# A 64-step recurrence on one core: from stationary weights to stationary tokens in four column tiles, with a new split between resident and streamed weights

## Chip, cores, metric

One core of one Trainium2 chip. The metric is the device time of one execution in microseconds, the median of four runs. The program uses one core, and all runs named here were in the undisturbed (fast) state.

## The reference

The output is `g * a + (1 - g) * b` for 2048 tokens of width 1024. `b` is a feed-forward network with gate, width 3584. `g` is a sigmoid per token. `a` is a recurrence: 64 segments of 32 tokens are taken in order, and each is joined with 8 memory tokens that the segment before it produced.

```python
for s in range(64):
    xs = x[:, s*32:(s+1)*32]
    h = concat([mem, xs])                      # 40 tokens x 1024
    q, k, v = h @ Wq, h @ Wk, h @ Wv           # 32 heads of 128 -> 4096 columns each
    scores = q k^T / sqrt(128), masked         # 40 x 40 per head
    o = softmax(scores) v
    o = o @ Wo                                 # 4096 -> 1024
    mem = o[:8];  outs.append(o[8:])
```

The four weight matrices hold 33.5 MB in bf16. Every segment needs all of them and neither kernel keeps all of them on chip, so every segment streams some of them again. Only the 8 memory tokens tie one segment to the next: queries, keys and values of the 32 input tokens could be computed earlier, and outputs of tokens that feed no memory could be computed later.

One warning about correctness: the recurrence is a tiny part of the output. With `Wo` set to zero, the reference changes by 5.6e-6 on average, where its mean magnitude is 3.8e-3. The comparison with the reference therefore cannot judge the recurrence. So no run here shows that the recurrence of the changed kernel is computed right.

## The kernel before

Weights are the stationary operand (loaded ahead of each matmul, 128x128 values), and the 40 tokens move through it. Wq, Wo and a part of Wk stay in SBUF, the on-chip memory. Wv and the rest of Wk are streamed each segment through a ring of three slabs of 1 MB (four heads, rows of 1 KB).

```python
def emit_slab(i):                              # SP queue, in order
    ...
    slot = i % RING                            # RING = 3
    waits = [(S_QKV_DONE, slab_free_target[i - RING])]
    E("sp", lambda e: e.dma_start(ring[:, slot, :, :], slab_src(kind, hq)), ...)

# Q, K, V: 96 blocks of 8 matmuls per segment, weights 128x128 stationary, 40 columns moving
for kc in range(KC):
    ins = e.matmul(PB[bank][:, bi*L:(bi+1)*L], lhsT=lhs_list[kc],
                   rhs=hT[:, cur, kc, :], start=(kc == 0), stop=(kc == KC - 1))
...
# output projection, 8 x 32 matmuls per segment
for kc in range(H):
    ins = e.matmul(dst_bank[:, fl*L:(fl+1)*L], lhsT=wo_sb[:, kc, f*128:(f+1)*128],
                   rhs=oT_sb[:, kc, :], start=(kc == 0), stop=(kc == H - 1))
```

After the recurrence, the feed-forward part works through 8 row groups of 256 tokens. It streams gate and up weights from SP's queue, and fetches each group's recurrence output with one DMA from POOL's queue:

```python
E("pool", lambda e: e.dma_start(a_sb[:, :, :],
    a_scr[r0:r0 + RG*128, :].rearrange("(t p) f -> p t f", p=128)), waits=aw, inc=(S2_ALD, 16))
```

Of the kernel before, what the change touches and what calls it, by code (L numbers as in the profile page):

```python
# [5 lines left out]
BF16 = mybir.dt.bfloat16  # L6
FP32 = mybir.dt.float32
# [4 lines left out]

class _Sem:

    def __init__(self, h):
        self.h = h
        self.n = 0


class _Gen:  # L20
# [3 lines left out]
    def __init__(self):  # L24
        self.prog = {e: [] for e in self.ENGS}

    def emit(self, eng, mk, waits=(), inc=None):
        waits = tuple((s.h, int(t)) for (s, t) in waits if t > 0)
        if inc is not None:
            s, k = inc  # L30
            s.n += k
            inc_h = (s.h, k)
        else:
            inc_h = None

        def run(e, mk=mk, waits=waits, inc_h=inc_h):
            for sh, t in waits:
                e.wait_ge(sh, t)
            ins = mk(e)
            if inc_h is not None:  # L40
                ins.then_inc(inc_h[0], inc_h[1])

        self.prog[eng].append(run)

    def wait_only(self, eng, sem, target):
        if target <= 0:
            return

        def run(e, sh=sem.h, t=int(target)):
            e.wait_ge(sh, t)  # L50

        self.prog[eng].append(run)

    def materialize(self, block):
        prog = self.prog

        if prog["sp"]:
            @block.sync
            def _(e):
                for f in prog["sp"]:  # L60
                    f(e)

        if prog["pool"]:
            @block.gpsimd
            def _(e):
                for f in prog["pool"]:
                    f(e)

        if prog["pe"]:
            @block.tensor  # L70
            def _(e):
                for f in prog["pe"]:
                    f(e)

        if prog["act"]:
            @block.scalar
            def _(e):
                for f in prog["act"]:
                    f(e)

        if prog["dve"]:
            @block.vector
            def _(e):
                for f in prog["dve"]:
                    f(e)


def bass_gated_mix__memory_aug_recurrent_mem_tr__geglu_ffn__prompt_kernel(
# [17 lines left out]
    Dw, H, Dh = A_Wq.shape  # L106
    assert Dw == D and Dh == 128
    M = A_mem0.shape[1]
    SEG = 32
    assert M == 8  # L110
    L = M + SEG
    NSEG = S // SEG
    KC = D // 128
    F = H * Dh
    FF = B_w_gate.shape[1]
    NJ = FF // 128
    assert FF % 128 == 0 and D % 128 == 0 and S % 128 == 0
    NF = D // 128
    scale = float(Dh) ** -0.5
    NEG = -30000.0  # L120

# [3 lines left out]
    HG = 8 if H % 8 == 0 else H  # L125
    NG_ATT = H // HG
    assert H % 4 == 0
    NQG = H // 4

    KRES_H = min(H, 12)  # L130
    KRES_H -= KRES_H % 4
    RING = 3

    gen_all_sems = []

    with ExitStack() as es_top:
        cnt = [0]

        def new_sem(name):
            cnt[0] += 1  # L140
            h = es_top.enter_context(nc.semaphore(f"{name}_{cnt[0]}"))
            return _Sem(h)

        a_scr = nc.dram_tensor("a_scr_rows", [S, D], BF16)

        with ExitStack() as es:
            tcnt = [0]

            def SB(shape, dt, name):
                tcnt[0] += 1  # L150
                return es.enter_context(nc.sbuf_tensor(f"{name}_{tcnt[0]}", list(shape), dt))

            def PS(shape, dt, name):
                tcnt[0] += 1
                return es.enter_context(nc.psum_tensor(f"{name}_{tcnt[0]}", list(shape), dt))

            assert HG == 8 and NG_ATT * 8 == H, "v2 chain assumes 8-head attention groups"
            RING = 3
            hT = SB([128, 2, KC, L], BF16, "hT")
            stage = SB([128, D], BF16, "stage")  # L160
            qkvT = SB([128, 2, 24, L], BF16, "qkvT")
            v_sb = SB([L, 2, HG, 128], BF16, "vsb")
            sm = SB([L, 2, HG, L], FP32, "sm")
            pn = SB([L, 2, HG, L], BF16, "pn")
            mx = SB([L, 2], FP32, "mx")
            nmx = SB([L, 2], FP32, "nmx")
            rsum = SB([L, 2, HG], FP32, "rsum")
            rrec = SB([L, 2, HG], FP32, "rrec")
            pT_sb = SB([L, 2, HG, L], BF16, "pT")
            oT_sb = SB([128, H, L], BF16, "oT")  # L170
            a_evac = SB([128, NF, SEG], BF16, "aev")
            ident = SB([128, 128], BF16, "ident")
            mask = SB([L, HG, L], BF16, "mask")
            wq_sb = SB([128, KC, F], BF16, "wq")
            wo_sb = SB([128, H, D], BF16, "wo")
            ring = SB([128, RING, KC, 512], BF16, "ring")
            avail = nc.sbuf_bytes_remaining - 2048
            KRES_H = min(H, 4 * (avail // (KC * 512 * 2)))
            KRES_H = max(0, KRES_H - KRES_H % 4)
            kres_sb = SB([128, KC, max(KRES_H, 4) * 128], BF16, "kres") if KRES_H > 0 else None  # L180

            PB = [PS([128, 512], FP32, f"pb{i}") for i in range(8)]
            PBV = [PB[i][:, :].bitcast(BF16) for i in range(8)]

            S_CONST = new_sem("const")
            S_XLOAD = new_sem("xload")
            S_WQ = [new_sem(f"wq{i}") for i in range(H // 4)]
            S_KRES = [new_sem(f"kr{i}") for i in range(max(1, KRES_H // 4))]
            S_WO = new_sem("wo")
            S_SLOT = [new_sem(f"slot{i}") for i in range(RING)]  # L190
            S_QKV_DONE = new_sem("qkvdone")
            S_QKV_EVAC = new_sem("qkvevac")
            S_PINIT = new_sem("pinit")
            S_XTR_DONE = new_sem("xtrdone")
            S_HT = new_sem("htready")
            S_VTR_DONE = new_sem("vtrdone")
            S_VTR_EVAC = new_sem("vtrevac")
            S_SC_DONE = new_sem("scdone")
            S_SMRD = new_sem("smrd")
            S_NMX = new_sem("nmx")  # L200
            S_EXP = new_sem("exp")
            S_PN = new_sem("pn")
            S_PT_DONE = new_sem("ptdone")
            S_PT_EVAC = new_sem("ptevac")
            S_O_DONE = new_sem("odone")
            S_O_EVAC = new_sem("oevac")
            S_WO_DONE = new_sem("wodone")
            S_WOEV = new_sem("woev")
            S_ATR_DONE = new_sem("atrdone")
            S_ASTG = new_sem("astg")  # L210
            S_ASTORE = new_sem("astore")
            S_DVE_L = new_sem("dvel")
            S_POOL_L = new_sem("pooll")

            g = _Gen()
            E = g.emit

            E("pool", lambda e: e.memset(ident[:], 0.0), inc=(S_POOL_L, 1))
            E("pool", lambda e: e.affine_select(out=ident[:], in_=ident[:], compare_op=ALU.not_equal,
                                                fill=1.0, base=0, pattern=[[-1, 128]], channel_multiplier=1),  # L220
              waits=[(S_POOL_L, S_POOL_L.n)], inc=(S_CONST, 1))
            E("pool", lambda e: e.memset(mask[:], 0.0), inc=(S_POOL_L, 1))
            E("pool", lambda e: e.affine_select(
                out=mask[:, :, 0:SEG], in_=mask[:, :, 0:SEG], compare_op=ALU.is_ge,
                fill=NEG, base=0, pattern=[[0, HG], [-1, SEG]], channel_multiplier=1),
              waits=[(S_POOL_L, S_POOL_L.n)], inc=(S_POOL_L, 1))
            E("pool", lambda e: e.memset(mask[SEG:L], 0.0), waits=[(S_POOL_L, S_POOL_L.n)], inc=(S_CONST, 1))
            CONST_ALL = S_CONST.n

            E("pool", lambda e: e.dma_start(stage[32:64, :], xf[0:SEG, :]), inc=(S_XLOAD, 16))  # L230
            E("pool", lambda e: e.dma_start(stage[64:64 + M, :], mem0[:, :]), inc=(S_XLOAD, 16))

            chunk_plan = []
            for gq in range(NG_ATT - 1):
                chunk_plan.append((list(range(8 * gq, 8 * gq + 4)), ("k", "q", "v")))
                chunk_plan.append((list(range(8 * gq + 4, 8 * gq + 8)), ("k", "q", "v")))
            gL = NG_ATT - 1
            chunk_plan.append((list(range(8 * gL, 8 * gL + 6)), ("k", "q")))
            chunk_plan.append((list(range(8 * gL + 6, 8 * gL + 8)), ("k", "q")))
            chunk_plan.append((list(range(8 * gL, 8 * gL + 8)), ("v",)))  # L240
            NCH = len(chunk_plan)

            def chunk_blocks(ci):
# [804 lines left out]
```

## Time and profile before

| | before |
|---|---|
| time, median (range) | 4275.2 us (4262.6 to 4291.5) |
| period of a segment (63 periods) | 55.1 us |
| of it: TensorE busy / waiting for the ring / "issue" | 40.6 / 8.6 / 3.5 us |
| granted TensorE clock in the recurrence | 0.73 |
| streamed per segment | 12 slabs, 12.6 MB |
| a feed-forward row group | 75.7 us |

The page of the profiled run, with the engines' busy time and the span in 40 slices (digits are tenths):

```profile
PE 3214.3 (75%) x79512; PEld 2888.8 (68%) x79512; DVE 1113.6 (26%) x2577; ACT 933.5 (22%) x3010; POOL 82.0 (2%) x165
...
PE   3777777777777777677777777777777775899998
...
PEclk7777777767777777776776777777777776899999
DMA  9777777777777777677777777777777776666665
GB/s 326 223 224 238 224 238 231 235 232 234 234 238 241 241 232 233 217 237 225 240 233 230 231 228 233 231 241 241 241 241 225 237 235 205 204 212 207 207 207 167
```

No engine and no queue is full: TensorE is busy for about 0.7 of the recurrence, its granted clock is 0.73 of full on average, and the DMA queue moves about 233 GB/s at 0.74 of its time. (In the clock records the value is 1.0 or 0.5, nothing between; a mean of 0.73 says that TensorE ran at half clock for about 54% of the time.) When something is serial, one has to look inside a segment. The timeline of the kernel before (start, duration, engine, line, operation, count, and in brackets the idle time before and what ended it):

```profile
2003.90 0.36 PE L615 MATMUL pb_21<-hT,wq 128*128 128x40 bf16 x8
2004.10 0.36 PE L615 MATMUL pb_21<-hT,ring 128*128 128x40 bf16 x8
...
2008.82 0.23 PE L615 MATMUL pb_21<-hT,wq 128*128 128x40 bf16 x3
2011.98 0.33 PE L615 MATMUL pb_21<-hT,wq 128*128 128x40 bf16 x5 [2.93 <-issue]
...
2026.47 0.71 PE L615 MATMUL pb_20<-hT,ring 128*128 128x40 bf16 x16 [2.36 <-DMA ring<-in_A_Wv_dram]
```

Eight pairs of weight load and matmul start every 0.206 us at full clock, 25.7 ns each. At 2008.8 TensorE stops for 2.9 us with no wait that the profile shows ("issue"). Late instructions are the likely cause, though not proved: the packed trace has a 16 KB transfer on an instruction queue from 2009.4 to 2010.5. In 58 of the 71 such gaps of over 1 us between 200 and 2600 us a transfer of this kind ends inside the gap, mostly 1.3 to 1.5 us before TensorE goes on (a stretch of that length holds such an end by chance about half the time). At 2026 it has waited 2.4 us for a slab.

Two feed-forward row groups, in the chain that ended last, restricted to a window around them (start, duration, what):

```profile
4113.22 1.23 DVE dsb L992
...
4188.96 1.23 DVE dsb L992
```

The first subtraction of each row group comes 75.74 us after that of the last one.

### The profile page before, as it was taken

The page shows a single profiled execution, that of the slowest core. Times are in us where ns is not written, and L with a number is a line of the kernel's source. Part 1 is how long each engine was busy: PE and PEld are TensorE (multiplying, and loading weights), DVE is VectorE, ACT ScalarE, POOL GpSimd, SP SyncE. Part 2 cuts the span into 40 slices and gives each one's busy share as a digit, 9 for nine tenths or more (in the row PEclk, how much of TensorE's full clock was granted, in tenths as well). Part 3 has the DMA queues.
Part 4 walks back from the last instruction along what each step waited for, and adds up shares of the span by engine and source line. Part 5 has one row for each costly group of instructions (what it writes and reads, how often), then busy time and mean ns, then how long its engine had stood idle before and what let it go on. Part 6 is the DMA issues. An engine that isn't in the chain of part 4 may idle for free. (4 is left out here: it accounts for less than half of the span.)

```text
span 4275.1 us, 169326 instructions
## 1 busy us (share of the span) xinstructions
PE 3214.3 (75%) x79512; PEld 2888.8 (68%) x79512; DVE 1113.6 (26%) x2577; ACT 933.5 (22%) x3010; POOL 82.0 (2%) x165
## 2 busy tenths in 40 slices
PE   3777777777777777677777777777777775899998
PEld 3666666667666666666666666666766765677776
DVE  1122222222222222122222222222222221455555
ACT  1122222222222222122222222222222221232222
POOL 0000000000000000000000000000000000000000
PEclk7777777767777777776776777777777776899999
DMA  9777777777777777677777777777777776666665
GB/s 326 223 224 238 224 238 231 235 232 234 234 238 241 241 232 233 217 237 225 240 233 230 231 228 233 231 241 241 241 241 225 237 235 205 204 212 207 207 207 167
DMA packets 945190, 982.94 MB, mean 230 GB/s; under 512 B 17256, under 2 KB 930664, under 8 KB 944496
## 3 DMA queue, kind: packets, MB, share of 16 engines
q1 hardware_dynamic: 937904, 955.31, 70.2%
q0 software_dynamic: 6592, 16.81, 1.2%
q8 instruction: 627, 10.27, 1.0%
q14 instruction: 67, 0.55, 0.0%
HBM read 963.66 MB, written 8.39 MB: 227 GB/s over the span
## 5 line engine op out<-in xcount | busy, mean ns | idle before, releaser
L615 PE MATMUL pb_21<-hT,ring 128*128 128x40 bf16 x12288 | 557.9, 192 | 331.7 <-DMA ring<-in_A_Wv_dram 197.2
L615 PE MATMUL pb_20<-hT,ring 128*128 128x40 bf16 x12288 | 555.7, 192 | 315.6 <-DMA ring<-in_A_Wv_dram 173.6
L615 PEld LDWEIGHTS pb_21<-hT,ring 128*128 128x128 bf16 x12288 | 449.9, 105 | 359.4 <-DMA ring<-in_A_Wv_dram 207.1
L615 PEld LDWEIGHTS pb_20<-hT,ring 128*128 128x128 bf16 x12288 | 448.7, 104 | 349.6 <-DMA ring<-in_A_Wv_dram 183.9
L615 PE MATMUL pb_20<-hT,wq 128*128 128x40 bf16 x8192 | 402.5, 189 | 23.6 <-issue 23.3
L615 PE MATMUL pb_21<-hT,wq 128*128 128x40 bf16 x8192 | 401.4, 189 | 15.4 <-issue 15.1
L641 ACT ACTIVATE qkvT<-pb_21 128x160 bf16<-128x160 f32 (+3 forms) x736 | 179.4, 310 | 909.4 <-PE pb_21 L615 909.0
L641 ACT ACTIVATE qkvT<-pb_20 128x160 bf16<-128x160 f32 (+3 forms) x736 | 179.4, 310 | 890.6 <-PE pb_20 L615 890.2
L410 DVE SCALAR_TENSOR_TENSOR sm<-pb_25,mask 40x320 f32<-40x320 f32 x128 | 61.8, 483 | 1173.0 <-PE pb_25 L399 1173.0
L615 PEld LDWEIGHTS pb_20<-hT,wq 128*128 128x128 bf16 x8192 | 312.3, 102 | 24.8 <-issue 24.5
L615 PEld LDWEIGHTS pb_21<-hT,wq 128*128 128x128 bf16 x8192 | 311.9, 102 | 19.7 <-issue 19.4
L678 PE MATMUL pb_27<-oT,wo 128*128 128x40 bf16 x8192 | 277.3, 199 | 46.7 <-issue 33.0
L678 PE MATMUL pb_26<-oT,wo 128*128 128x40 bf16 x8192 | 256.3, 190 | 73.1 <-issue 73.1
L678 PEld LDWEIGHTS pb_27<-oT,wo 128*128 128x128 bf16 x8192 | 268.4, 109 | 55.1 <-issue 34.7
L678 PEld LDWEIGHTS pb_26<-oT,wo 128*128 128x128 bf16 x8192 | 246.5, 103 | 77.4 <-issue 77.2
L550 DVE COPY stage<-pb_22 32x1024 bf16<-32x1024 bf16 x64 | 43.5, 679 | 933.8 <-PE pb_22 L543 933.8
L969 PE MATMUL psB<-wd,GT 128*128 128x512 bf16 x896 | 228.7, 379 | 16.8 <-DVE GT L950 16.8
L451 PE MATMUL pb_23<-ident,qkvT 128*40 128x128 bf16 x2048 | 226.3, 278 | 15.0 <-issue 5.4
L907 PE MATMUL psh<-xTall,ringb 128*128 128x256 bf16 x1792 | 233.8, 274 | 0.6 <-DVE gall L870 0.6
L917 PE MATMUL psh<-xTall,ringb 128*128 128x256 bf16 x1792 | 233.2, 273 | 0.0
L907 PEld LDWEIGHTS psh<-xTall,ringb 128*128 128x128 bf16 x1792 | 176.0, 98 | 65.8 <-issue 0.6
L615 PE MATMUL pb_21<-hT,kres 128*128 128x40 bf16 x4096 | 192.0, 183 | 27.0 <-issue 17.7
(78 smaller groups left out, 3379.0 us busy)
## 6 DMA issues: line engine op xcount, KB each, us to landing
ring<-in_A_Wv_dram SPq DMA_DIRECT2D x512, 1024.0 KB, 6.1
ring<-in_A_Wk_dram SPq DMA_DIRECT2D x256, 1024.0 KB, 6.5
ringb<-in_B_w_gate_dram SPq DMA_DIRECT2D x56, 1024.0 KB, 5.2
ringb<-in_B_w_up_dram SPq DMA_DIRECT2D x56, 1024.0 KB, 7.8
wq<-in_A_Wq_dram SPq DMA_DIRECT2D x8, 1024.0 KB, 11.9
wo<-in_A_Wo_dram SPq DMA_DIRECT2D x8, 1024.0 KB, 13.9
wd<-in_B_w_down_dram SPq DMA_DIRECT2D x7, 1024.0 KB, 7.5
kres<-in_A_Wk_dram SPq DMA_DIRECT2D x4, 1024.0 KB, 11.6
```

The source lines that it names most:

```text
L410: E("dve", lambda e, b=b: e.scalar_tensor_tensor(out=sm[:, b, :, :], in0=PB[5 + b][0:L, 0:8 * L].rearrange("p (h k) -> p h k", h=8), scala ...
L451: ins = e.transpose(PBV[3][0:L, i * 128:(i + 1) * 128], qkvT[:, slot, 16 + i, :], ident[:, :])
L550: E("dve", lambda e: e.tensor_copy(stage[0:SEG, :], PBV[2][0:SEG, 0:D]), waits=dw, inc=(S_ASTG, 1))
L615: ins = e.matmul(PB[bank][:, bi * L:(bi + 1) * L], lhsT=lhs_list[kc], rhs=hT[:, cur, kc, :], start=(kc == 0), stop=(kc == KC - 1))
L641: E("act", lambda e, v3=v3, slot=slot, mi=mi, m=m, hh0=hh0, nh=nh: e.activation(qkvT[:, slot, midx[m] * 8 + hh0:midx[m] * 8 + hh0 + nh, :] ...
L678: ins = e.matmul(dst_bank[:, fl * L:(fl + 1) * L], lhsT=wo_sb[:, kc, f * 128:(f + 1) * 128], rhs=oT_sb[:, kc, :], start=(kc == 0), stop=(k ...
L907: ins = e.matmul(ps_h[:, hb, 0:RG * 128], lhsT=ringb[:, i_g % RINGB, kc, col:col + 128], rhs=xT_all[:, kc, rows], start=(kc == 0), stop=(k ...
L917: ins = e.matmul(ps_h[:, hb, RG * 128:2 * RG * 128], lhsT=ringb[:, i_u % RINGB, kc, col:col + 128], rhs=xT_all[:, kc, rows], start=(kc == ...
L969: ins = e.matmul(ps_B[:, t * NHALF + hf, 0:WH], lhsT=GT[:, gb, t * 128:(t + 1) * 128], rhs=wd_sb[:, j, hf * WH:(hf + 1) * WH], start=(j == ...
```

## The change

The intent: use fewer and longer matmuls in the recurrence. The stationary operand is now a block of 32 tokens by 128 inputs. 24 of a segment's 32 input tokens ride along with the 8 memory tokens, which makes 32. The other 8 of each segment are projected four segments at a time (32 again): Q, K and V before the first of the four, the output projection after the last. A stationary operand of 32 columns fills one column tile of four, so four matmuls stand side by side, each with another quarter of the weight columns moving through it.

```diff
-for kc in range(KC):
-    e.matmul(PB[bank][:, bi*L:(bi+1)*L], lhsT=lhs_list[kc], rhs=hT[:, cur, kc, :], ...)
+def quad(s, mat, u, bank, rbank):              # twice for each of Q, K, V
+    for kc in range(KC):
+        w = piece(s, p)                        # [128, 2048] of the weights: resident, or a ring slot
+        for st, bk in ((h, bank), (xR, rbank)):      # xR: the 32 batched tokens, first segment of four
+            for g in range(4):
+                e.matmul(PB[bk][32*g:32*g+32, :], lhsT=st[:, kc, :], rhs=w[:, g*512:(g+1)*512],
+                         start=(kc == 0), stop=(kc == KC - 1))
+        consumed(s, p)                         # emits the next ring load on SP's queue
...
-for kc in range(H): e.matmul(dst_bank[...], lhsT=wo_sb[:, kc, f*128:(f+1)*128], rhs=oT_sb[:, kc, :])
+# output projection: 16 pieces x 2 heads x 4 column tiles of 256 columns
+for g in range(4):
+    e.matmul(PB[0][32*g:32*g+32, 0:256], lhsT=oT[:, a, gp, 0:32], rhs=w[:, c:c+256], ...)
```

The weights are cut into 64 pieces of 0.5 MB, in rows of 4 KB (Wo: 2 KB). 41 stay resident and 23, spread evenly over all four matrices, go through a ring of five slots: 12.1 MB per segment. Queries and keys come out with tokens on partitions, so they must be copied and transposed before the scores; the softmax is reordered as well. Semaphore waits are no longer written by hand: a tracker derives them from the byte ranges and PSUM banks that each operation declares. The loads of the recurrence output for the feed-forward part moved to SP's queue:

```diff
-E("pool", lambda e: e.dma_start(a_sb[:, :, :], a_scr[r0:r0 + RG*128, :]...), waits=aw, ...)
+def load_a(rg):
+    for t in range(RG):
+        for i in range(4):
+            op("sp", ... e.dma_start(asb[t][32*i:32*i+NR, :], a_main[4*T+i, :, :]),
+               wr=[asb[t].r()], lane=f"al{t}_{i}")
+            op("sp", ... e.dma_start(asb[t][32*i+NR:32*i+32, :], a_rest[T, 8*i:8*i+8, :]),
+               wr=[asb[t].r()], lane=f"am{t}_{i}")
```

(Cut: the attention, the front end that writes transposed inputs to scratch memory, and the feed-forward part, whose matmuls are the same as before.)

## The prediction

> **What bounds the kernel now.** By the windows view the recurrence takes 3600 us (64 segments of 55.9 us), then a 55 us front end and about 615 us of feed-forward. A segment streams 12 slabs of 1 MB. A saturated queue moves 349 GB/s with these 1 KB rows (5 us windows), so slabs need 36 us; the queue is 73% busy. The timeline shows why: during the output projection (256 pairs, 7 to 10 us) and the attention tail the three-slab ring is full and the DMA idle; during Q, K, V TensorE waits for slabs (`ring`, about 600 us in the waits view) and "issue" (gaps near 3 us, some 300 us). TensorE issues 1024 weight-load/matmul pairs of 128x40 per segment, 25.7 ns each at full clock, 33 at half; granted clock 0.73. A segment is a poorly overlapped sum of 36 us of DMA and 27 to 34 us of matmuls.
>
> **What the change does.** Weights move, 32 tokens are stationary, in four column tiles: per segment 48 groups of four 512-column matmuls and 32 groups of four 256-column ones; batched tokens add 48 groups in the first segment of four and 32 in the last. Feed-forward matmuls run at 0.41 ns per column, so a group costs 0.21 us (0.11 us) only if the four tiles run together. No trace here shows that; the Trainium skill, "TensorE: Matmul & The Clock Gate", Part 3, measured 2.38x for three column tiles. I count 0.22 and 0.13 us.
>
> Streamed bytes hardly change: 23 pieces of 0.52 MB, 12.1 MB. Rows become 4 KB; before, 2 KB rows ran at 387 GB/s, so I take 395: 30.6 us. The stream is now spread over all projections, so it overlaps better.
>
> Estimated segment without batch, full clock: Q, K, V 10.7 us; transposes 0.5; copies, second transpose and POOL copy before the scores 2.9; 128 score matmuls with masks 3.8; denominator, Ln, subtract, Exp, V copy 2.4 (trace: 0.48 us per 320-element DVE pass, 0.56 per Exp); PV 1.8; its copies 1.2; output projection 4.2; return of memory 1.2: 29 us. Batch: +12 in one segment, +4 in another; mean 33. The five-piece ring adds about 2 us of DMA waits; engine-to-engine gaps keep the clock from staying full (+4), instruction fetch +1.5, tile mode switches +0.5: about 41 us. Critical path: TensorE plus the serial attention steps, DMA just beneath.
>
> Sum: front transposes and scratch writes 50; first segment, bound by 33 MB of weights, 88; 63 x 41 = 2580; start of feed-forward 45 (15 MB before the gate matmuls); 612 for the rest, unchanged. About 3375; I say 3350.
>
> **Prediction: 3350 us, 3000 to 3750 in 8 of 10 cases. Faster by over 2%: 0.94; within 2%: 0.02; slower: 0.04.**
>
> **What would show it.** Timeline: the four tiles' matmuls start within some 10 ns of each other, groups every 0.21 us at full clock. DMA: recurrence near 300 GB/s, 385 to 405 saturated. Segments 36 to 46 us, batching ones 10 us longer. Clock 0.75 to 0.9. Waits: two attention gaps of 2 to 3 us per segment, a few us of ring waits. Feed-forward row groups stay at 75.7 us.
>
> **What would make it wrong.** Column tiles that run one after another (192 x 0.21 us for Q, K, V alone): over 5000 us. Half clock most of the time: segments near 50 us. Small weight loads that can't hide behind matmuls. A POOL copy much over 0.6 us, or SP's in-order queue holding ring loads behind stores. The other way: full clock throughout gives 36 us per segment, near 3050 us.

## The result and the profile after

3640.3 us (3634.6 to 3642.2) against 4275.2 us. The ratio of the fast runs is 0.8495, with a 95% interval of 0.8462 to 0.8527. A ratio here and below is the mean time of one kernel's fast runs over that of the other's of the same rounds, so it is not quite the ratio of the medians quoted.

| per segment, mean of 56 segments | before | after |
|---|---|---|
| period | 55.1 | 43.3 us |
| TensorE busy | 40.6 | 29.3 |
| TensorE waits for ring pieces | 8.6 | 4.8 |
| waits for the batched tokens (`xR`) | - | 1.5 |
| "issue" | 3.5 | 1.1 |
| waits for copies, transposes and softmax steps | 2.2 | 6.6 |

The lower four rows are TensorE's waits in the waits view over the same 56 segments, divided by 56. The period is measured between the first and last instance of one instruction, over 63 segments. Periods of the recurrence fell by 11.8 us. The feed-forward part went the other way: from the end of the recurrence to the end of the span, 675 us (3600 to 4275) became 789 us (2848 to 3637).

The page of the changed kernel:

```profile
PE 2512.6 (69%) x44606; PEld 1401.3 (39%) x44678; DVE 800.5 (22%) x1873; ACT 565.3 (16%) x1315; POOL 115.9 (3%) x348
...
PE   3667666666666666767676666766666488888887
...
PEclk9688888988888788878887988888888699999998
DMA  8987887888787978787887888787978655555554
GB/s 300 357 288 270 281 295 278 305 282 306 258 314 255 317 255 312 265 292 270 303 281 271 309 278 287 262 312 260 305 264 318 240 174 173 174 173 174 173 174 126
```

TensorE executes 44606 matmuls instead of 79512. Its granted clock rises in the recurrence. The last nine slices, the feed-forward part, have a lower TensorE share than before (8 against 9 tenths).

The timeline of one first segment of four in the changed kernel, TensorE only (hT: the 32 tokens of the segment; xR: the 32 batched ones; res and ring: resident and streamed pieces of weights):

```profile
2015.64 0.38 PE L612 MATMUL pb<-kT,qT 128*32 128x40 bf16 x32
2015.86 0.46 PE L618 MATMUL pb<-kT,qT 128*8 128x40 bf16 x32
2016.15 0.48 PE L624 MATMUL pb<-qT,kT 128*32 128x40 bf16 x32
2016.47 0.43 PE L630 MATMUL pb<-qT,kTB 128*32 128x16 bf16 x32
2016.74 0.41 PE L496 MATMUL pb<-res_116,hT_56 128*32 128x512 bf16 x4
2016.96 0.41 PE L496 MATMUL pb<-res_116,xR 128*32 128x512 bf16 x4
2017.17 0.41 PE L496 MATMUL pb<-ring_93,hT_56 128*32 128x512 bf16 x4
```

The L496 rows answer to the L615 rows before. A group is four matmuls of 512 columns on four tiles; the groups follow each other every 0.215 us, which is the time of 512 columns in one matmul. So the four tiles work together. The four rows above are the score matmuls, 128 of them in 1.10 us (2015.64 to 2016.74), 8.6 ns each.

Where the stream stands inside a segment, in windows of 2 us of the changed kernel (columns: stretch, its length, busy time and instruction count of TensorE, weight loads, DVE, ACT, POOL, granted clock, DMA share, GB/s):

```profile
2084.00:2086.00 2.00, 1.39 (x22) 0.36 (x23) 0.00 (x0) 0.00 (x0) 0.00 (x0) 1.00 1.03 414
2102.00:2104.00 2.00, 0.23 (x27) 0.13 (x16) 0.68 (x2) 0.87 (x2) 0.00 (x0) 0.73 1.05 401
2104.00:2106.00 2.00, 1.65 (x32) 1.23 (x36) 0.30 (x1) 0.00 (x0) 0.40 (x1) 0.50 0.55 198
2144.00:2146.00 2.00, 2.00 (x43) 1.31 (x39) 0.00 (x0) 0.00 (x0) 0.00 (x0) 0.50 0.02 3
```

At 2084, in the K projection, the queue is saturated at 414 GB/s while TensorE works 1.39 of 2 us. At 2144, in an output projection, the ring is full and the DMA idle. The clock falls to half at 2103, in the last of three idle gaps of TensorE from the end of the V projection to the output projection:

```profile
2099.02 0.40 PE L496 MATMUL pb<-ring_94,hT_56 128*32 128x512 bf16 x4 [1.63 <-DMA ring_94<-in_A_Wv_dram]
2101.57 0.37 PE L692 MATMUL pb<-EA,vA 32*128 32x40 bf16 x32 [1.85 <-DVE vA L521]
2104.36 0.62 PE L727 MATMUL pb<-res_126,oT 128*32 128x256 bf16 x8 [2.12 <-DVE oT L710]
```

Start of the next segment with batched tokens:

```profile
2153.01 0.47 SPq L470 DMA_DIRECT2D xR<-xb_scr  x1
2153.87 0.40 PE L496 MATMUL pb<-res_95,hT_56 128*32 128x512 bf16 x4 [0.28 <-DVE hT_56 L750]
2160.17 0.62 PE L496 MATMUL pb<-res_95,xR 128*32 128x512 bf16 x4 [5.90 <-DMA xR<-xb_scr]
```

TensorE does one group, then stops 5.9 us for the batched tokens. Their load was issued at 2153.0, behind five ring loads issued from 2147.5 to 2152.6. Over the 56 segments of the table the waits view counts 15 such stops (us in total, times, longest):

```profile
PE pb L496 <- DMA xR<-xb_scr: 84.8, 15, 7.4
```

A row group of the feed-forward part in the changed kernel, and SP's own waits (who waited for whom, us in total, times, longest):

```profile
3170.42 0.32 SPq L819 DMA_DIRECT2D asb_151<-a_main  x1
3172.93 0.29 SPq L821 DMA_DIRECT2D asb_151<-a_rest  x1
3174.53 0.29 SPq L819 DMA_DIRECT2D asb_151<-a_main  x1
3176.26 0.26 SPq L821 DMA_DIRECT2D asb_151<-a_rest  x1
...
3195.14 0.26 SPq L821 DMA_DIRECT2D asb_152<-a_rest  x1
...
3200.75 1.89 PE L848 MATMUL pb<-xT,rb_140 128*128 128x256 bf16 x8 [10.06 <-DMA rb_140<-in_B_w_gate_dram]
```

```profile
SPq L821 <- DMA asb_151<-a_main: 54.3, 32, 3.0
SPq L821 <- DMA asb_152<-a_main: 44.8, 32, 1.7
SPq L819 <- DMA asb_151<-a_rest: 34.1, 24, 2.9
SPq L819 <- DMA asb_152<-a_rest: 31.1, 24, 1.7
```

Sixteen small loads are issued from 3170.4 to 3195.1, eight for each of two tiles. Within a tile each waits for the one before it to land. Only then can SP issue the next slab of weights, and TensorE starts again at 3200.75, after 10 us of idling. The row group's period is 92.1 us here (first subtraction of each group, from 2984.27 to 3629.02, seven periods), not 75.7.

### The profile page after: what moved, and what is told of

The parts are those of the page before. It is cut to its first block, busy times and chain, and to the rows that moved or that the text cites. A ratio compares the mean times of both kernels' runs of the same rounds, so it can differ in the third digit from the quotient of the medians.

```text
span 3637.2 us, 95669 instructions
## 1 busy us (share of the span) xinstructions
PE 2512.6 (69%) x44606; PEld 1401.3 (39%) x44678; DVE 800.5 (22%) x1873; ACT 565.3 (16%) x1315; POOL 115.9 (3%) x348
## 4 chain that ended last, share of the span: by engine, by line
PE 44%; DMA 39%; DVE 7%; ACT 4%; issue 4%; SPq 1%; POOL 1%; ACTq 0%; POOLq 0%
PE pb L496 14%; PE pb L727 8%; PE pb L848 8%; PE pb L873 4%; DMA xR<-xb_scr 3%; DMA ring_91<-in_A_Wk_dram 3%; DMA ring_93<-in_A_Wk_dram 3%; DMA ring_92<-in_A_Wk_dram 3%; DMA ring_94<-in_A_Wk_dram 3%; PE pb L528 2%; DMA ring_90<-in_A_Wk_dram 2%; PE pb L733 2%; DMA ring_93<-in_A_Wq_dram 2%; DMA ring_91<-in_A_Wq_dram 2%; DMA ring_94<-in_A_Wq_dram 2%
## 5 line engine op out<-in xcount | busy, mean ns | idle before, releaser
L858 DVE SCALAR_TENSOR_TENSOR tp<-s_145,pb 128x256 f32<-128x256 f32 x224 | 94.2, 420 | 304.5 <-ACT s_145 L857 304.5
L848 PE MATMUL pb<-xT,rb_138 128*128 128x256 bf16 x896 | 124.7, 286 | 50.2 <-DMA rb_138<-in_B_w_gate_dram 50.2
L857 ACT ACTIVATE s_145<-pb 128x256 f32<-128x256 f32 x224 | 85.9, 383 | 452.8 <-PE pb L848 396.3
L848 PE MATMUL pb<-xT,rb_140 128*128 128x256 bf16 x896 | 122.6, 282 | 40.1 <-DMA rb_140<-in_B_w_gate_dram 40.1
L848 PE MATMUL pb<-xT,rb_139 128*128 128x256 bf16 x896 | 122.0, 281 | 5.6 <-DMA rb_139<-in_B_w_up_dram 5.6
L848 PEld LDWEIGHTS pb<-xT,rb_138 128*128 128x128 bf16 x896 | 91.3, 102 | 88.5 <-DMA rb_138<-in_B_w_gate_dram 52.4
L848 PE MATMUL pb<-xT,rb_141 128*128 128x256 bf16 x896 | 120.4, 279 | 4.5 <-DMA rb_141<-in_B_w_up_dram 4.5
L848 PEld LDWEIGHTS pb<-xT,rb_140 128*128 128x128 bf16 x896 | 90.3, 101 | 77.2 <-DMA rb_140<-in_B_w_gate_dram 42.1
L861 DVE SCALAR_TENSOR_TENSOR g_147<-tp,pb 128x256 f32<-128x256 f32 x224 | 94.4, 422 | 108.9 <-ACT tp L860 108.9
L860 ACT ACTIVATE tp<-tp 128x256 f32<-128x256 f32 x224 | 93.2, 416 | 115.8 <-DVE tp L858 115.8
L848 PEld LDWEIGHTS pb<-xT,rb_139 128*128 128x128 bf16 x896 | 89.8, 101 | 20.4 <-DMA rb_139<-in_B_w_up_dram 8.0
L541 DVE COPY qT<-pb 128x1024 bf16<-128x1024 bf16 x64 | 44.3, 692 | 242.0 <-PE pb L528 242.0
L848 PEld LDWEIGHTS pb<-xT,rb_141 128*128 128x128 bf16 x896 | 89.2, 100 | 18.2 <-DMA rb_141<-in_B_w_up_dram 6.4
L541 DVE COPY kT<-pb 128x512 bf16<-128x512 bf16 (+1 forms) x112 | 51.7, 461 | 179.8 <-PE pb L528 179.8
L710 DVE CAST oT<-pb 128x320 bf16<-128x320 f32 x128 | 62.9, 492 | 121.4 <-ACT oT L708 121.4
L873 PE MATMUL pb<-wd,GT_149 128*128 128x512 bf16 x273 | 73.2, 388 | 13.4 <-DVE GT_149 L863 11.6
```

Source lines behind the costliest of these rows:

```text
L541: op("dve", lambda e: e.tensor_copy(o_ap, i_ap), rd=[BK(bank)], wr=[reg])
L848: ins = e.matmul(PB[hb][:, half * 256:(half + 1) * 256], lhsT=w[:, kc, c:c + 128], rhs=xT[:, rg * RG:(rg + 1) * RG, kc, :], start=(kc == 0 ...
L857: op("act", lambda e: e.activation(s1[:, :], hg, ACTF.Square, scale=SQ), rd=[BK(hb)], wr=[s1.r()])
L858: op("dve", lambda e: e.scalar_tensor_tensor(out=tp[:, :], in0=s1[:, :], scalar=1.0, in1=hg, op0=ALU.add, op1=ALU.mult), rd=[BK(hb), s1.r( ...
L860: op("act", lambda e: e.activation(tp[:, :], tp[:, :], ACTF.Tanh, scale=C_GELU), rd=[tp.r()], wr=[tp.r()])
L861: op("dve", lambda e: e.scalar_tensor_tensor(out=g1[:, :], in0=tp[:, :], scalar=1.0, in1=hu, op0=ALU.add, op1=ALU.mult), rd=[BK(hb), tp.r( ...
```

## The experiments

Two questions: what did the gain come from, and what keeps the changed kernel 290 us above the prediction? Unless said otherwise the edits are made in the changed kernel, whose time is 3640 us; "per segment" is counted as in the table above.

### a_serial: the four tiles parted

```diff
+tl = g if kc == 0 else 0
-e.matmul(PB[bk][32*g:32*g+32, :], lhsT=st[:, kc, :], rhs=w[:, g*512:(g+1)*512], ...)
+e.matmul(PB[bk][32*tl:32*tl+32, :], lhsT=st[:, kc, :], rhs=w[:, g*512:(g+1)*512], ...)
```

> Changing the order of the matmuls did not part the column tiles: each tile worked off its own matmuls. So the parting is forced: in Q, K and V the last seven of eight input blocks use one column tile for all four matmuls (wrong result on purpose; same matmuls, columns and bytes). If the four tiles working together are what makes the change pay, such a group takes 0.85 instead of 0.213 us: 33 us more per segment, some 5 us of it hidden in ring waits: total 5200 to 5600, slower than before. Rival (TensorE's gain comes from fewer, longer matmuls): under 4275.

Measured: 5194.3 us (ratio to before 1.216), just under the range given. The timeline of this kernel:

```profile
2300.52 1.03 PE L497 MATMUL pb<-res,xR 128*32 128x512 bf16 x4
2301.38 1.03 PE L497 MATMUL pb<-res,hT 128*32 128x512 bf16 x4
```

A group takes 0.86 us, four times 0.215. A segment grows by 24.3 us to 67.5: TensorE's busy time by 29.9 us, while ring waits fall to almost nothing. So the change pays only if the tiles work together. Without that, with the same number of matmuls, it is 22% slower than the old kernel; fewer and longer matmuls alone are not the gain.

Their length matters all the same, as the traces show. Per segment both kernels do the same multiply-adds in the projections: 1024 matmuls of 40 columns before, and after, on average, 60 groups of 512 and 40 of 256 columns, which is 40960 columns of the full array in both. At full clock 40 columns took 25.7 ns (0.64 ns per column), a group of 512 columns 0.215 us (0.42 ns). That makes about 26 and 17 us per segment at full clock, an estimate from these two durations. In the score matmuls, where the columns are 40, groups of four tiles start 25 to 34 ns apart in the packed trace: side by side, but short, they do no more per microsecond than the old pairs. The gain needs both, four tiles to keep the array full and long streams through it. No run varied the length alone with the work kept.

### a_pair: another order of the same matmuls

```diff
-for kc:  for g in range(4):  matmul(tile g, block kc)
+for pairs of kc:  for g in range(4):  for d in range(2):  matmul(tile g, block 2*k2+d)
```

> The changed kernel, with the same matmuls in another order in Q, K and V: for each column tile two input blocks after each other, then the next tile (right result). If the four tiles run together only when neighbouring matmuls go to different tiles, eight matmuls take five slots of 0.213 us instead of two: 19 us more per segment, less the ring waits that this hides, total 4400 to 4850. Rival (the gain does not rest on tiles running together, or the queue reorders them): within 3% of 3640.

Measured: 3658.2 us, 0.5% above the changed kernel. My expectation failed, the rival held. The timeline of this kernel:

```profile
2022.34 0.41 PE L498 MATMUL pb<-ring,hT 128*32 128x512 bf16 x4
2022.56 0.40 PE L498 MATMUL pb<-res,hT 128*32 128x512 bf16 x4
2022.78 0.40 PE L498 MATMUL pb<-ring,xR 128*32 128x512 bf16 x4
```

In the program, each tile's `ring` matmul is followed by the same tile's `res` matmul, before the next tile's. In the trace the four `ring` matmuls run together, then the four `res` matmuls. So the tiles work off their matmuls independently, over at least eight instructions, and the order of neighbours need not be interleaved by hand. (The trace does not hold the order in which instructions were issued; that it is the program's order is assumed.)

### b_halfdma: half the stream in the kernel before

```diff
-e.dma_start(ring[:, slot, :, :], slab_src(kind, hq))
+e.dma_start(ring[:, slot, 0:kk, :], slab_src(kind, hq)[:, 0:kk, :])     # kk = 4 of 8 after the first three
```

> The kernel before, with the slab loads after the first three bringing only half the rows (wrong result on purpose). It asks how much of the old time was waiting for the stream. Theory: 10 to 12 us of each 55.9 us segment; ring waits vanish and the issue gaps stay, total 3450 to 3650 - so the old kernel without DMA limit would be about where the changed one is with it. Rival (the old kernel was bound by its 1024 pairs and its fetch gaps): less than 200 us gained, total over 4070.

Measured: 3622.9 us, 652 us less than before. A segment falls from 55.1 to 45.0 us: ring waits from 8.6 to 3.5 us, "issue" from 3.5 to 0.9 us, TensorE's busy time from 40.6 to 38.1 us at a clock of 0.82 instead of 0.73. The expectation held in the total. About 40% of the ring waits stayed, so "vanish" was too strong, and "issue" did not stay. The windows view over 56 segments, first of the kernel before, then of b_halfdma:

```profile
288.00:3375.40 3087.40, 2274.21 (x65446) 2126.28 (x65442) 684.14 (x1624) 660.13 (x2240) 55.59 (x112) 0.73 0.74 233
246.00:2763.60 2517.60, 2131.03 (x65558) 2000.49 (x65555) 684.79 (x1625) 660.05 (x2243) 55.97 (x113) 0.82 0.46 146
```

With half the stream, "issue" and the time at half clock fell as well, so the stream's price here was more than the waits put down to the ring. How the stream brings these about, the run does not show.

### a_halfdma and a_halfdma2: half the stream in the changed kernel

```diff
-e.dma_start(dst(t, p), src(p))
+e.dma_start(dst(t, p)[0:64], src(p)[0:64])               # a_halfdma: 64 of 128 partitions
+e.dma_start(dst(t, p)[:, 0:1024], src(p)[:, 0:1024])     # a_halfdma2: half of each row (Wo: one of two heads)
```

> The changed kernel, with the ring loads after the first five bringing only 64 of the 128 partitions (wrong result on purpose: the other half is stale). It asks what the stream costs in the recurrence. Theory (segment = serial TensorE work and attention chain, plus about 5 us of ring waits): ring waits vanish, segment about 38 us, total 3290 to 3400. Rival (the stream bounds the recurrence): segments shrink towards 33 us or less, total under 3150.

Measured: 3411.1 us, 11 us above the range. But the run doesn't answer the question: ring waits stayed at 3.8 us per segment. The windows view of a_halfdma:

```profile
1000.00:1180.00 180.00, 126.12 (x2956) 67.68 (x2960) 34.06 (x80) 27.03 (x64) 7.44 (x19) 0.90 0.75 162
```

The queue is busy 0.75 of the time for 162 GB/s; in the 2 us windows where it is saturated (DMA share 1.0 or more, 1000 to 1800 us) it moves 205 GB/s in the median, the changed kernel 397. At these rates a piece of half the partitions (262 KB) takes 1.28 us and a whole one (524 KB) 1.32 us: so the edit halved the bytes but hardly the time that a piece takes. The segment is 3.5 us shorter all the same: 1.6 us of TensorE's busy time, at a clock of 0.90 in place of 0.85, 1.0 of ring waits, 0.6 of waits for the batched tokens, 0.5 of "issue". What brought this about stays open.

> Halving the partitions did not take the stream away (the queue stayed 73% busy and ring waits stayed at 3.9 us per segment), so the question is asked again: the changed kernel, with the ring loads after the first five bringing half of each row to all 128 partitions (2 KB rows, wrong result on purpose). Theory (a segment is serial TensorE work and attention chain, plus 4.8 us of ring waits): ring waits under 1 us per segment, segment 37 to 39 us, total 3250 to 3400. Rival (the stream bounds the recurrence): segment under 34 us, total under 3100.

Measured: 3133.4 us, 507 us less, between the two ranges; neither theory was right in size. A segment takes 35.0 us, 8.2 less. Ring waits fall by 3.2 us to 1.5, waits for the batched tokens by 1.05, "issue" by 0.7. The other 3.3 us are TensorE's busy time, 26.0 instead of 29.3, for the same matmuls. The windows view, first of the changed kernel, then of a_halfdma2, on the same stretch:

```profile
1000.00:1180.00 180.00, 120.52 (x2542) 58.52 (x2540) 28.96 (x67) 23.60 (x54) 6.22 (x16) 0.84 0.82 283
```

```profile
1000.00:1180.00 180.00, 133.48 (x3194) 72.33 (x3186) 37.33 (x86) 29.47 (x68) 8.53 (x22) 0.94 0.60 190
```

The clock is 0.94 here instead of 0.84 (over 56 segments 0.92 and 0.85). Halving the stream thus saves 8.2 us per segment, more than the 4.8 us that are named after it, and with 1.5 us of ring waits left. A higher clock comes with fewer waits here; that the waits lower it is likely but not isolated.

With the stream halved in both kernels, the segment is 45.0 us before and 35.0 us after; with the whole stream, 55.1 and 43.3. So about 10 of the 11.8 us that a segment gained are gained with the stream eased too. It is not gone in either: 3.5 and 1.5 us of ring waits are left, and without these the difference is 8.0 us.

### a_halfpe: less matmul work

```diff
+NW = 512 if kc in (0, KC - 1) else 256
-e.matmul(PB[bk][32*g:32*g+32, :],    ..., rhs=w[:, g*512:(g+1)*512], ...)
+e.matmul(PB[bk][32*g:32*g+32, 0:NW], ..., rhs=w[:, g*512:g*512+NW], ...)
```

> The changed kernel, with six of the eight matmul groups of each Q, K and V projection only 256 columns wide (wrong result on purpose): 4.8 us less of TensorE work per segment, same DMA. Theory (TensorE and stream both bind, by turns): 1 to 3 us less per segment, total 3450 to 3580, ring waits grow by what is not gained. Rival 1 (TensorE bound): the full 4.8 us, total 3330. Rival 2 (stream bound): within 1%.

Measured: 3582.0 us, 58 less, 2 us above the first theory's range. Ring waits grow by 2.1 us per segment. TensorE's busy time falls by only 2.35 us instead of 4.8, because the granted clock in these segments falls from 0.85 to 0.71. Both together take back most of the saving, so less matmul work alone would gain little in this kernel.

### a_1kb: short rows

```diff
+sr = W[kc*128:(kc+1)*128].rearrange("d (x hh) e -> d x (hh e)", hh=4)[:, u:8:2, :]
-e.dma_start(dst(t, p), src(p))
+e.dma_start(t[:, :].rearrange("p (x c) -> p x c", x=4), sr)       # Q, K, V pieces
```

> The changed kernel, with the ring loads of the Q, K and V pieces in rows of 1 KB from scattered heads (same bytes, wrong result on purpose); the 4 KB rows are part of the change. At 349 instead of 410 GB/s a piece takes 1.50 instead of 1.28 us: 3.8 us more per segment for 17 pieces if the stream is on the path all along, about 2.5 us if in part: total 3740 to 3880. Rival (row size does not matter here): within 1% of 3640.

Measured: 3704.0 us, 64 more, under my range and over the rival's. Saturated 2 us windows show 350 GB/s in the median in place of 397, near what was assumed, but ring waits grow by only 1.05 us per segment: presumably the longer transfers fall in part into times when the ring would have been full. The 4 KB rows contribute about 1 us per segment.

### a_nobatch: the matmul time without batching

```diff
-for st, bk in ((h, bank), (xR, rbank)):
+for st, bk in ((h, bank), (xR, rbank) if rbank is not None else (h, bank)):   # start/stop flags adapted
```

> The changed kernel, with every Q, K and V matmul group issued twice in the three segments of four that have no batched tokens (wrong result on purpose). It stands for the same kernel without batching[...]. TensorE work grows by 7.7 us per segment on average; ring waits of 4 to 5 us hide part: total 3800 to 4050. Rival (the stream hides all of it, batching gains nothing): within 2% of 3640.

The stand-in costs as much TensorE work as if the 8 other tokens had their own set of groups in every segment.

Measured: 3748.4 us, 108 more: clear of the rival but under my range. TensorE's busy time grows by only 5.3 us per segment, with the clock at 0.91, and ring waits fall from 4.8 to 1.6 us. The segment is 1.9 us longer. Batching the projections is worth about 3% of the time as the kernel stands; the stand-in leaves out what batching saves in the output projection.

### fix_a: the loads of the recurrence output no longer wait for each other

```diff
+rec_end = [o for o in P.ops if o.eng == "pe"][-1]
-   wr=[asb[t].r()], lane=f"al{t}_{i}")
+   wr=[("A", t, i, 0)], lane=f"al{t}_{i}", after=[rec_end])
-   wr=[asb[t].r()], lane=f"am{t}_{i}")
+   wr=[("A", t, i, 1)], lane=f"am{t}_{i}", after=[rec_end])
-rd=[BK(b), asb[t].r()]
+rd=[BK(b)] + [("A", t, i, h) for i in range(4) for h in range(2)]
```

> The changed kernel, but the sixteen loads that bring a row group's recurrence output for the feed-forward part no longer wait for each other (each writes its own part of the tile and is tracked so). Theory: in the changed kernel SP's in-order queue is held by these loads, each waiting for the one before to land, so the weight slabs behind them come late: row groups of 92 us instead of 75.7. Expected: row groups back to 75 to 78 us, total 90 to 130 us less than 3640 (about 3525). Rival: the feed-forward part is slower because its operands or PSUM tracking changed (bank-wide waits); then the total stays within 20 us of 3640.

Measured: 3522.9 us, 117 less. Row groups take 78.6 us (3113.73, 3192.34, ... in the chain of this kernel), near 75.7 but not quite. The windows view from the first feed-forward matmul after the gate to the end of the span, first the changed kernel, then fix_a (columns as in the windows above):

```profile
2899.60:3637.20 737.60, 609.34 (x4381) 444.56 (x4450) 322.49 (x731) 176.41 (x445) 0.00 (x0) 0.92 0.53 166
```

```profile
2890.40:3519.70 629.30, 588.87 (x4382) 437.76 (x4451) 323.29 (x731) 176.06 (x445) 0.00 (x0) 0.98 0.62 194
```

The same work takes 629.3 us instead of 737.6. That is 108 of the 117.5 us by which the profiled span fell; the recurrence, which the edit does not touch, ended 9 us earlier in this run, and the cause of that stays open. The tracker knows byte ranges within a partition but not partitions. Two loads into different partitions of one tile looked to it like two writes to the same bytes, and it made SP wait for the first to land.

### fix_xr: the batched tokens loaded early

```diff
 quad(s, "v", 1, *bv[1])
+if R and s + 4 < NSEG:
+    load_xR(G + 1)
...
-if not last:
-    load_xR(G + 1)         # after the last segment of the four
```

> The changed kernel, with the load of the next 32 batched tokens issued right after the last projection that reads the old ones (first segment of four) instead of after the last segment of the four. Theory: TensorE waits 5.7 us for this load in 15 segments because it stands behind five ring loads in the DMA queue. Expected: that wait gone, total 60 to 100 us less (about 3555). Rival: the wait only hides ring waits that then appear in its place, as the ring fills meanwhile; then less than 30 us.

Measured: 3527.1 us, 113 less, more than expected. The wait is gone. Ring waits per segment stay as they were (4.9 us), so the rival failed. The clock rises from 0.85 to 0.87 and TensorE's busy time falls by 0.55 us: the 5.7 us stop may also have cost clock.

### st_act: stores from ACT's queue

```diff
-op("sp",  lambda e, g=g: e.dma_start(a_main[s, :, g*256:(g+1)*256], ab[32*g:32*g+NR, :]), ...)
+op("act", lambda e, g=g: e.dma_start(a_main[s, :, g*256:(g+1)*256], ab[32*g:32*g+NR, :]), ...)
```

(and likewise `a_rest`)

> The changed kernel, with the stores of each segment's output issued from ACT's queue instead of SP's. Theory: SP spends 1.6 us per segment (4.1 us in one of four) issuing stores, while ring slots are free and wait to be refilled; this causes part of the 5 us of ring waits per segment. Expected: 50 to 150 us less (about 3540), no gap of over 2 us between ring issues while a slot is free. Rival: the ring waits come from the bandwidth of the queue; then within 30 us of 3640.

Measured: 3592.6 us, 48 less, a little under the range. Ring waits fell by only 0.25 us per segment. So the stores were a small part of the ring waits. Bandwidth in the bursts of the Q and K projections is left as the likely larger one; no run tested it directly.

### all3

The three edits above together.

> The three edits together. If they add up: 220 to 380 us less than 3640, about 3340, and a segment of about 40.5 us. If ring bandwidth is what is left underneath, less than the sum of the three.

Measured: 3366.2 us (3360.2 to 3368.7), ratio to before 0.787. That is 274 less than the changed kernel; the three alone sum to 278. A segment takes 40.8 us. This is the fastest version without a deliberate error that was run.

## Why the prediction was right, and where it was off

The time fell in the range and the direction held, but 3640 is 290 us above 3350. The three over-runs below come to 277 us (145 in the segments, 126 in the row groups, 6 in the front); 3375 had been rounded down to 3350, and start and first segment took about 122 us where 138 were given. Point by point:

- **Four tiles together, 0.22 us a group: right.** Measured 0.215 us at full clock. The Trainium skill, "TensorE: Matmul & The Clock Gate", Part 3, reports 2.38 for three column tiles; in a long stream this case shows the full factor of four (0.86 against 0.215 us in a_serial). Its sentence "`pack_span ≈ MM_dur + (ntile − 1) × ~4ns`", which gives an estimate of about 3.8 for four tiles of 0.215 us, is nearer than the measured factor beside it. The four starts of a group lie 7 to 9 ns apart in the packed trace, not 4.
- **Score matmuls, 3.8 us with masks: too high.** With masks they take 1.7 us (2015.07 to 2016.74), because column tiles overlap these short matmuls too (8.6 ns each).
- **Segment of 41 us: measured 43.3, about 145 us over 63 segments.** The term "the five-piece ring adds about 2 us of DMA waits" was mis-sized: 4.8 us. The term for the batched tokens' load, 1.5 us per segment, was missing altogether. Waits of TensorE on softmax, copies and transposes are 6.6 us, where two gaps of 2 to 3 us had been expected. That the sum came so near is partly luck: 2.1 us too much for the scores stood against 2.8 us too little for the ring and the missing 1.5. The clock, 0.85, was in the range given; 285 GB/s is near the 300 given.
- **"612 for the rest, unchanged": wrong, by 126 us.** The feed-forward row groups took 92.1 us instead of 75.7, and from the end of the gate matmuls (2899.6) to the end of the span it is 738 us, 126 more than I gave. The matmuls were indeed unchanged; SP's queue was not. I had named "SP's in-order queue holding ring loads behind stores" as a danger, but looked for it in the recurrence and not in the sixteen loads of each row group. fix_a shows the cause of 108 of these 126 us: with it, this part takes 629 us. The other 17 (row groups of 78.6 instead of 75.7 us) were not traced.
- **Front of the feed-forward part, 45 us: measured about 51 us** (2848 to 2899.6).
- **What gained.** Per segment, TensorE's busy time fell by 11.3 us, ring waits by 3.9, "issue" by 2.4, while the serial attention steps gave back 4.3 and the batched tokens 1.5. The prediction called the old segment a poorly overlapped sum of stream and matmuls. That was right (b_halfdma: 652 us), but it does not mean that the gain came from a better stream: the bytes are the same, the long rows are worth about 1 us, and 8 to 10 us of the 11.8 remain with the stream halved. By the estimate under a_serial, long matmuls on a full array save TensorE some 9 us per segment at full clock.

What stays open: the tracker makes ACT and DVE take turns on the four attention output copies, which all declare the whole `oT` tile (TensorE waits 1.6 us per segment for the last of them), and on copies that only read different halves of one PSUM bank. Both look like false dependences of the same kind as in fix_a; no run took them away. A deeper ring, or more streamed pieces in the output projection and fewer in Q and K, was not tried either. At half clock a long matmul takes twice its time (eight 256-column matmuls of the output projection follow each other every 0.43 us at 2105, every 0.22 us at 2110), but how much of the waits' price this makes can't be separated here; a_halfdma2 shows the sum.

## What to carry to other kernels

If a recurrence has few tokens, make them the stationary operand and put them in column tiles side by side, and let long rows of weights stream through them. Check in the trace that a group of four takes the time of one. When waits come from a tracker instead of by hand, look at every in-order queue for loads that wait on each other: a declaration that is too coarse for the tile made nothing fail and cost 108 us. Price a stream by taking it away, not by the waits that carry its name: here halving it saved 8.2 us, where 4.8 us of waits were named after it.

## What the Trainium skill lacked or had wrong

- "TensorE: Matmul & The Clock Gate", Part 3, states that matmuls are strictly in program order in start and end. In a_pair the starts are not in program order across column tiles (four `ring` matmuls at 2022.34, then four `res` matmuls at 2022.56, although they alternate in the program).
- "TensorEngine Tiling (Array Packing)", Performance Considerations, Instruction Overhead, gives each matmul an overhead of about 60 cycles and leaves open whether column tiles bear it side by side. Here they do: 128 matmuls of 40 and 16 columns in column tiles took 8.6 ns each; untiled pairs with 40 columns took 25.7 ns in the kernel before.
- "TensorE: Matmul & The Clock Gate", closing table, asks for no idle gaps over about 3 us. Shorter gaps are no safe side: in the changed kernel the clock fell to half at 2103 us, after idle gaps of 1.6 and 1.9 us and within one of 2.1 us, with about 0.7 us of matmuls between them. In a_halfpe it was 0.71 on average although of TensorE's waits only those for the ring grew, by 2.1 us per segment.
- "DMA: Bandwidth & Descriptors", Rules for kernel authors, advises 128 partitions and at least 1 MiB per DMA. The first half is borne out: loads of 64 partitions in 4 KB rows saturated at 205 GB/s in the median. The second half was not needed: with pieces of 0.5 MB in rows of 4 KB the queue moved 404 to 414 GB/s in the windows from 2084 to 2092 us (median of the saturated windows 397).
